# Block means of the first batch spread by POOL for both heads, and four weight pairs converted with the attention's priority

## Chip, cores, metric

One core of one Trainium2 chip runs the whole program. The time is device microseconds of one launch, median of the runs. Beside it stands one profiled execution, from which all rows below come. The engines are PE (TensorE: matmuls into PSUM), DVE (VectorE), ACT (ScalarE), POOL (GpSimd) and SP, which issues the DMAs.

## What is computed

For 4 batches: attention with 8 heads over 768 positions (head size 64), in which each query sees its neighbours within 16 positions and, beside them, 24 blocks of 32 positions: the maximum of each block's keys and the mean of its values. A mixer then works on the result (768 x 512 a batch): a product along the positions (768 to 256 to 768) that is added to its input, and one along the channels (512 to 1536 to 512) that is added again.

```python
k_sum = k.reshape(B, H, nb, block, D).max(axis=3)
v_sum = v.reshape(B, H, nb, block, D).mean(axis=3)      # the block means of this case
scores_l = where(|i - j| < 16, scale * q @ k.T, -1e9)
scores_s = scale * q @ k_sum.T + log(block)
a = softmax(concat([scores_l, scores_s]))
x = a @ concat([v, v_sum])                              # heads side by side: 768 x 512
u = x + (relu(x.T @ w_tok1) @ w_tok2).T
out = u + relu(u @ w_ch1) @ w_ch2
```

## The kernel before

**Stages.** Batch 0's attention runs alone in a start stage. Heads go in pairs `p` = 0 to 3: scores `sc` on PE, their lowest value on DVE (L481), the exponential `e` on ACT (L491), transposes `et` on PE, weighted sums `av` on PE, scaled by DVE into `x` (L610). Each pair's `x` goes through the first token product (`tok1`: PE into `t1p`, then ACT and DVE into `t1`, L734 and L739) and the second (`tok2`: PE into `up`, then ACT and DVE into `u`, L959 and L964). `u_0_1_2` is batch 0, second half of the positions, channel block 2. When the start is over, PE goes through a long stream of channel products, `hp` (L981, `ch1`) and `acc` (L1024, `ch2`), 24 steps a batch, with the attention of the next batch between the steps.

**Weights.** Single-precision weights are used as the sum of two shorter numbers, high and low, and are made on the chip in the start stage and the first stream. `w_tick(i)` takes pair `i`: two loads by SP, then ACT's absolute value (L1665), POOL's clamp (L1669), and on DVE a shift (L1674), a sign (L1681) and the low word (L1688); then, but for the first token weight, ACT writes the high part (L1712) and POOL subtracts to get the low part (L1718), twice each. Pairs 0 to 2 are `w_tok1` (tile `wt1`), 3 to 5 are `w_tok2` (`wb_3` to `wb_5`, into `wt2h` and `wt2l`), 6, 8, ... are `w_ch1` (`w1h`, `w1l`), 7, 9, ... are `w_ch2`. `tok2` needs all of 3 to 5; the stream's first step needs pair 6.

**Block means of batch 0.** `first_means(p)`: PE sums the 32 rows of each block in two parts for both heads into one PSUM bank (`vm`, tag `acc2`, of which there is one), ACT copies one part into `vs` (L372), DVE adds the other (L382), and 24 x 64 means must stand twelve times beside the values `v` as 24 x 768.

**Order.** Nothing is issued in the order of the code. Every piece of work is listed by `add(engine, estimated time, ..., rank)`, and `Plan._order` plays the list through with these estimates: each engine takes the ready piece of lowest rank, then of lowest place in the list. What comes out is a fixed order for each engine's queue; on the chip each engine keeps it and waits on semaphores. The ranks are `R_H, R_EVAC, R_ATT, R_LATER, R_W` = 0 to 4.

Of the kernel before, what the change touches and what calls it, by code (L numbers as in the profile page):

```python
# [15 lines left out]
ALU = mybir.AluOpType  # L16
# [3 lines left out]
B, H, S, D = 4, 8, 768, 64  # L20
# [5 lines left out]
NT = S // QT  # L26
NB = S // 32
WIN = 96
NC = WIN + NB
# [49 lines left out]
class Plan:  # L79
# [13 lines left out]
    def add(self, eng, took, run, reads=(), writes=(), rank=0, behind=(), kb=0):  # L93

        w = Work(len(self.works), eng, took, run, rank, kb)
        self.works.append(w)
        for key in reads:
            if key in self.wrote:
                w.needs.add(self.wrote[key])
            self.read[key].append(w)  # L100
        for key in writes:
            if key in self.wrote:
                w.needs.add(self.wrote[key])
            w.needs.update(self.read.pop(key, ()))
            self.wrote[key] = w
        for key in (*reads, *writes):
            s = getattr(key[0], "home", key[0])
            if isinstance(s, Slot) and (not s.users or s.users[-1] is not w):
                if not s.users:
                    w.takes.append(s)  # L110
                s.users.append(w)
        w.behind.update(behind)
        w.needs.discard(w)
        return w
# [85 lines left out]
def tile_attention_mixer(  # L200
# [13 lines left out]
    nc = tc.nc  # L214
# [6 lines left out]
    add = plan.add  # L221

    def sbuf(shape, tag, name, bufs, dtype=F32):
        return plan.slot(sb, shape, dtype, tag, name, bufs)
# [10 lines left out]
        out=means[:, NB - 2 : NB],  # L235
# [4 lines left out]
        out=means[:, NB - 2 : NB], in0=means[:, NB - 2 : NB], scalar1=1.0 / 32.0,  # L240
# [23 lines left out]
    R_H, R_EVAC, R_ATT, R_LATER, R_W = range(5)  # L264
# [11 lines left out]
    def bank(name, tags):  # L276
        tag = tags[turns[tuple(tags)] % len(tags)]
        turns[tuple(tags)] += 1
        return plan.slot(ps, [P, 512], F32, tag, name, 2 if tag in ("att", "mm") else 1)
# [8 lines left out]
    q_t, k_t, v_t, vs, vb_t = {}, {}, {}, {}, {}  # L288
# [62 lines left out]
    def first_means(p):  # L351

        pt = bank(f"vm_{p}", ["acc2"])
        s = sbuf([P, 2 * D], "vs", f"vs_0_{p}", 2)


        def sums():
            for t in range(NT):
                for j in range(2):
                    c = 2 * j + t % 2  # L360
                    nc.tensor.matmul(
                        pt.t[32 * c : 32 * c + NB, :D],
                        lhsT=means[:, NB - 2 - 2 * t : 2 * NB - 2 - 2 * t],
                        rhs=v_t[2 * p + j].t[:WIN, t], start=(t < 2), stop=(t >= NT - 2),
                    )

        def half(j, i):
            c = 2 * j + i
            return pt.t[32 * c : 32 * c + NB, :D]

        def first(j):
            nc.scalar.activation(s.t[WIN:NC, j * D : (j + 1) * D], half(j, 0), AF.Copy)  # L372

        def both(n):
            nc.vector.tensor_tensor(
                out=v_t[n].t[WIN:NC],
                in0=half(1, 1).unsqueeze(1).broadcast_to([NB, NT, D]),
                in1=s.t[WIN:NC, D:].unsqueeze(1).broadcast_to([NB, NT, D]), op=ALU.add,
            )

        def once():
            nc.vector.tensor_tensor(  # L382
                out=s.t[WIN:NC, :D], in0=half(0, 1), in1=s.t[WIN:NC, :D], op=ALU.add
            )

        def spread(n):
            nc.gpsimd.tensor_copy(
                v_t[n].t[WIN:NC], s.t[WIN:NC, :D].unsqueeze(1).broadcast_to([NB, NT, D])
            )

        add(
            "pe", 0.9, sums, reads=[(v_t[2 * p], 0), (v_t[2 * p + 1], 0)], writes=[(pt, 0)],
            rank=R_H,
        )
        for j in range(2):
            add(
                "act", 0.25, lambda j=j: first(j), reads=[(pt, 0)], writes=[(s, j)], rank=R_EVAC
            )
        add("dve", 0.2, once, reads=[(pt, 0)], writes=[(s, 0)], rank=R_EVAC)
        add(  # L400
            "pool", 0.95, lambda: spread(2 * p), reads=[(s, 0)], writes=[(v_t[2 * p], 1)],
            rank=R_ATT,
        )
        add(
            "dve", 0.95, lambda: both(2 * p + 1), reads=[(pt, 0), (s, 1)],
            writes=[(v_t[2 * p + 1], 1)], rank=R_EVAC,
        )

    def vb_load(b, c):
        tag, n, bufs = ("e", 16, 3) if b == 1 else ("vb", 8, 1)  # L410
# [233 lines left out]
    def att_step(b, s, behind=()):  # L644

        kind, hp, g = (LATER if b >= FAR else ORDER)[s]
        p = b * NP + hp
        if kind == "e":
            (turn_blocks if b >= FAR else turn)(p, g)
        elif kind == "a":  # L650
            weighted(p)
            if b >= FAR:
                turn_x(b, hp)
            ahead = 1 if b > 0 else 2
            if b > 0 or hp + ahead < NP:
                load_v(2 * (p + ahead))
                load_v(2 * (p + ahead) + 1)
        else:
            scores(p, g, behind)
            if b == 0 and g == 1:  # L660
                first_means(p)
            if g == 0 and p != NP - 1:
                key_blocks(p + 1)
            if g == 1 and p + 2 < (NP if b == 0 else B * NP):
                load_k(p + 2)
                state["q"] = load_q(p + 2)
# [929 lines left out]
    for i in range(3):  # L1596
        for k in range(2):
            cs, ws = slice(256 * i, 256 * (i + 1)), slice(512 * i, 512 * (i + 1))
# [12 lines left out]

    BUFS = {"u0": 4, "q": 2, "k": 2, "v": 2, "x": 2, "h": 2}
    ROOM = {"u0", "k", "h", "x"}
    TOKT = 3
    WTAGS = ["u0"] * 6 + ["k", "k", "q", "v", "x", "x"] * 4
    assert 2 * len(WTAGS) == len(jobs)

    def w_tick(i, behind=()):
# [12 lines left out]
        for j in range(2):  # L1631
# [7 lines left out]
            )  # L1639
        first, rank = two[0][1] is None, R_ATT if i < TOKT else R_W  # L1640
        psum = i >= 10
# [105 lines left out]
    for s in range(STEPS):  # L1747
# [4 lines left out]
        if ORDER[s][0] == "a":  # L1752
            p = ORDER[s][1]
# [143 lines left out]
```

## Time and profile before

| | |
|---|---|
| median of 3 runs | 560.84 us (560.51 to 561.32) |
| the profiled execution, its own time | 559.61 us |
| its span in the profile | 557.8 us |
| granted TensorE clock | 1.00 over the span |
| busy: PE, DVE, ACT, POOL | 544.0, 330.3, 251.9, 246.8 us |

The span is what the profile shows between the first and the last instruction; 1.8 us lie around it. A busy share is an average over stages: the start (to some 64 us) and the stream behind it have different limits. PE's busy time counts matmuls that overlap, so it is no measure of what could still be saved.

### The profile page before, as it was taken

How to read it: one execution, taken by the hardware profiler on the slowest of the kernel's cores; microseconds unless marked ns; L12 is line 12 of the kernel's file. 1: busy time of each engine (PE TensorE's matmuls, PEld its weight loads, DVE VectorE, ACT ScalarE, POOL GpSimd, SP SyncE). 2: the span in 40 equal slices, each digit the busy share in tenths (PEclk: the TensorE clock that was granted, in tenths of full speed). 3: DMA queues.
4: the chain of work that ended last, by engine and by line, in shares of the span. 5: the costliest groups of instructions: out<-in, count | busy, mean ns of one | idle time of the engine just before them, and what ended most of it. 6: DMA issues, size and time to landing. Idle time of an engine off the chain costs nothing.

```text
span 557.8 us, 12595 instructions
## 1 busy us (share of the span) xinstructions
PE 544.0 (98%) x4557; PEld 479.6 (86%) x4557; DVE 330.3 (59%) x922; ACT 251.9 (45%) x784; POOL 246.8 (44%) x362
## 2 busy tenths in 40 slices
PE   7699999999999999999999999999999999999997
PEld 4588788888999978888799988878889999999997
DVE  4788999979365355454543247454352065669992
ACT  4786666625585344332323325343433453356410
POOL 0326687835574932310067404378769963000000
PEclk9999999999999999999999999999999999999999
DMA  8963668755668138768595316787696543932742
GB/s 277 330 189 108 215 209 249 240 163 190 203 187 251 42 131 226 198 207 226 146 253 137 104 29 196 160 237 198 171 259 168 135 155 116 333 95 81 219 134 85
DMA packets 125743, 101.10 MB, mean 181 GB/s; under 512 B 70000, under 2 KB 105456, under 8 KB 125680
## 3 DMA queue, kind: packets, MB, share of 16 engines
q1 hardware_dynamic: 125680, 100.29, 60.7%
q8 instruction: 36, 0.59, 0.5%
q14 instruction: 27, 0.22, 0.1%
HBM read 70.18 MB, written 28.31 MB: 177 GB/s over the span
## 4 chain that ended last, share of the span: by engine, by line
PE 90%; ACT 4%; DVE 3%; POOL 2%; issue 1%; ACTq 0%
PE acc L1024 27%; PE hp L981 27%; PE sc L467 4%; PE av L599 4%; PE up L920 3%; PE t1q L837 3%; ACT e L491 2%; PE x L1251 2%; PE y L1251 2%; PE z L1251 2%; PE pz L1251 2%; PE t1q L800 2%; PE up L1213 2%; PE warm L1731 1%; PE pw L1251 1%; PE pv L1251 1%
## 5 line engine op out<-in xcount | busy, mean ns | idle before, releaser
L1024 PE MATMUL acc<-h,w2h 128*128 128x256 f32 (+1 forms) x576 | 153.8, 339 | 0.0
L981 PE MATMUL hp<-u,w1h 128*128 128x256 f32 (+1 forms) x576 | 143.8, 339 | 0.0
L1024 PEld LDWEIGHTS acc<-h,w2h 128*128 128x128 f32 x576 | 100.6, 188 | 13.8 <-ACT h L993 1.6
L981 PEld LDWEIGHTS hp<-u,w1h 128*128 128x128 f32 x576 | 98.0, 189 | 12.4 <-issue 1.1
L981 PE MATMUL hp<-u,w1l 128*128 128x256 f32 (+1 forms) x288 | 96.9, 336 | 0.0
L491 ACT ACTIVATE e<-e,den 128x120 f32<-128x120 f32 x192 | 73.3, 384 | 52.0 <-DVE den L481 39.1
L1024 PE MATMUL acc<-h,w2l 128*128 128x256 f32 (+1 forms) x288 | 96.4, 335 | 0.0
L998 DVE SCALAR_TENSOR_TENSOR h<-hp,h 128x512 fp32r<-128x512 f32 (+1 forms) x72 | 39.9, 554 | 90.9 <-ACT h L993 90.7
L993 ACT ACTIVATE h<-hp 128x512 fp32r<-128x512 f32 (+1 forms) x72 | 35.2, 489 | 114.7 <-PE hp L981 114.5
L981 PEld LDWEIGHTS hp<-u,w1l 128*128 128x128 f32 x288 | 54.4, 189 | 5.8
L1024 PEld LDWEIGHTS acc<-h,w2l 128*128 128x128 f32 x288 | 54.2, 188 | 5.2
L481 DVE CUSTOM_DVE_ANT_0 e<-sc,mask_sb 128x120 f32<-128x120 f32 x192 | 41.7, 277 | 16.8 <-PE sc L467 16.2
L605 POOL TENSOR_SCALAR rec<-den 128x6 f32<-128x6 f32 x32 | 8.6, 269 | 66.1 <-ACT e L491 64.0
L491 ACT ACTIVATION_READ_ACCUMULATOR e<-e,den 128x1 f32 x192 | 36.1, 188 | 0.0
L1064 POOL TENSOR_TENSOR ot<-ot,u 128x512 f32<-128x512 f32 (+1 forms) x24 | 24.4, 1042 | 19.7 <-DVE ot L1056 18.2
L467 PE MATMUL sc<-k,q 64*64 64x120 f32 x768 | 28.0, 271 | 3.7 <-DVE den L481 2.2
L467 PEld LDWEIGHTS sc<-k,q 64*64 64x64 f32 x768 | 20.5, 132 | 12.5 <-issue 6.2
L920 PE MATMUL up<-wt2h,t 128*128 128x512 f32 (+1 forms) x96 | 28.4, 354 | 0.6 <-DVE t L739 0.6
L599 PEld LDWEIGHTS av<-v,eT 120*64 120x64 f32 x768 | 24.0, 138 | 4.7 <-issue 2.8
L599 PE MATMUL av<-v,eT 120*64 120x64 f32 x768 | 26.5, 224 | 0.9 <-PE hp L981 0.4
L335 DVE TENSOR_REDUCE ks<-k 128x24 f32<-128x768 f32 x16 | 15.2, 948 | 20.5 <-DMA k<-in_kw 20.5
L423 DVE TENSOR_REDUCE vs<-vb 96x8 f32<-96x256 f32 (+1 forms) x40 | 17.8, 458 | 9.4 <-DMA vb<-in_vb 9.3
(248 smaller groups left out, 1042.7 us busy)
## 6 DMA issues: line engine op xcount, KB each, us to landing
w<-in_w_ch SPq DMA_DIRECT2D x48, 256.0 KB
k<-in_kw SPq DMA_DIRECT2D x16, 720.0 KB
v<-in_vw SPq DMA_DIRECT2D x32, 288.0 KB
q<-in_q SPq DMA_DIRECT2D x16, 384.0 KB
away<-e SPq DMA_DIRECT2D x16, 384.0 KB
eT<-away SPq DMA_DIRECT2D x64, 96.0 KB
w<-in_w_tok SPq DMA_DIRECT2D x12, 256.0 KB
vb<-in_vb SPq DMA_DIRECT2D x32, 96.0 KB
```

Source lines behind the costliest of these rows:

```text
L423: lambda: nc.vector.tensor_reduce(out=s.t[:VB, rows], in_=slot.t[:VB], axis=AX, op=ALU.add),
L467: nc.tensor.matmul(tiles[j].t[c * QT : (c + 1) * QT, i * NC : (i + 1) * NC], lhsT=qt.t[rows, t * QT : (t + 1) * QT], rhs=kt.t[rows, t, :], ...
L481: nc.vector.tensor_tensor_reduce(out=e.t[:, j, i * P : i * P + NC], in0=tiles[j].t[:, i * NC : (i + 1) * NC], in1=mask_sb[:, mv, :], op0=A ...
L491: nc.scalar.activation(ei, ei, AF.Exp, bias=den_t[n].t[:, 1, T : T + 1], scale=-1.0, accum_out=den_t[n].t[:, 0, T : T + 1],)
L599: nc.tensor.matmul(pv[cs, T], lhsT=eT[:NC, T % (TT // 2), cs], rhs=v.t[:NC, 2 * T + c], start=True, stop=True,)
L920: nc.tensor.matmul(pt.t[:, :nt], lhsT=t1.t[:, part, ks], rhs=w.t[:, k, h0 : h0 + nt], start=(far and k == 0 and i == 0), stop=(k == DTOK / ...
L981: nc.tensor.matmul(pt.t[:, :nt], lhsT=block(w, f, c), rhs=us[c].t[:, part], start=(i == 0), stop=(i == len(ops) - 1),)
L993: lambda: nc.scalar.activation(h.t[:, 0], pt.t[:, :nt], AF.Relu),
L998: lambda: nc.vector.scalar_tensor_tensor(out=h.t[:, 1], in0=pt.t[:, :nt], scalar=0.0, in1=h.t[:, 0].bitcast(F32), op0=ALU.max, op1=ALU.sub ...
L1024: nc.tensor.matmul(slot.t[:, c0 : c0 + nt], lhsT=block(w, f, o), rhs=h.t[:, part], start=(f == 0 and w == "w2h" and part == 0 and o % n == 0),
L1064: lambda view=view, u=u: nc.gpsimd.tensor_tensor(out=view(), in0=view(), in1=u.t[:, 1].bitcast(F32), op=ALU.add),
L1251: nc.tensor.matmul(pt.t[:, :cols], lhsT=w[wp][0](), rhs=z.t[:, zp], start=first and seen == 0, stop=final and seen == 3 * len(ops) - 1, sk ...
```

## The change

In `first_means` DVE no longer writes the second head's 24 x 768 itself (`both`, 24 x 768 from PSUM). It writes the 24 x 64 means of both heads (`once`), and POOL spreads both (`spread`, rank `R_ATT`). `TOKT` goes from 3 to 7: weight pairs 3 to 6 (the second token weight and the first pair of the first channel weight) get rank `R_ATT` in place of `R_W`, for all their steps on ACT, POOL and DVE.

```diff
-        def both(n):
+        def once(j):
+            cs = slice(j * D, (j + 1) * D)
             nc.vector.tensor_tensor(
-                out=v_t[n].t[WIN:NC],
-                in0=half(1, 1).unsqueeze(1).broadcast_to([NB, NT, D]),
-                in1=s.t[WIN:NC, D:].unsqueeze(1).broadcast_to([NB, NT, D]), op=ALU.add,
-            )
-        def once():
-            nc.vector.tensor_tensor(
-                out=s.t[WIN:NC, :D], in0=half(0, 1), in1=s.t[WIN:NC, :D], op=ALU.add
-            )
-        def spread(n):
+                out=s.t[WIN:NC, cs], in0=half(j, 1), in1=s.t[WIN:NC, cs], op=ALU.add
+            )
+        def spread(j):
             nc.gpsimd.tensor_copy(
-                v_t[n].t[WIN:NC], s.t[WIN:NC, :D].unsqueeze(1).broadcast_to([NB, NT, D])
+                v_t[2 * p + j].t[WIN:NC],
+                s.t[WIN:NC, j * D : (j + 1) * D].unsqueeze(1).broadcast_to([NB, NT, D]),
             )
...
-        add("dve", 0.2, once, reads=[(pt, 0)], writes=[(s, 0)], rank=R_EVAC)
-        add("pool", 0.95, lambda: spread(2 * p), reads=[(s, 0)], ..., rank=R_ATT)
-        add("dve", 0.95, lambda: both(2 * p + 1), reads=[(pt, 0), (s, 1)], ..., rank=R_EVAC)
+        for j in range(2):
+            add("dve", 0.2, lambda j=j: once(j), reads=[(pt, 0)], writes=[(s, j)], rank=R_EVAC)
+            add("pool", 0.95, lambda j=j: spread(j), reads=[(s, j)], ..., rank=R_ATT)
...
-    TOKT = 3
+    TOKT = 7
```

Since the order is played through anew, much of the start stage moves. Three places follow; line numbers of the changed kernel are 6 lower than before.

On DVE, at the means of pairs 0 and 1 (`vs_0_0`, `vs_0_1`; `e_1_1` are scores of pair 1, `ks_2` the block maxima of pair 2), before:

```order
L382 TENSOR_TENSOR vs_0_0_269<-vm_0_223,vs_0_0_269 24x64
L375 TENSOR_TENSOR v_1_89<-vm_0_223,vs_0_0_269 24x768
L481 ISA e_1_1_309,den_2_217<-sc_2_1_280,mask_sb_71 128x120
...
L610 TENSOR_TENSOR x_0_0_335<-av_0_296,rec_0_249 128x6x64
L335 TENSOR_REDUCE ks_2_363<-k_2_158 128x24
L610 TENSOR_TENSOR x_0_0_335<-av_1_318,rec_1_254 128x6x64
L382 TENSOR_TENSOR vs_0_1_376<-vm_1_338,vs_0_1_376 24x64
L375 TENSOR_TENSOR v_3_115<-vm_1_338,vs_0_1_376 24x768
```

and now:

```order
L376 TENSOR_TENSOR vs_0_0_269<-vm_0_223,vs_0_0_269 24x64 x2
L376 TENSOR_TENSOR vs_0_1_320<-vm_1_279,vs_0_1_320 24x64 x2
L604 TENSOR_TENSOR x_0_0_343<-av_0_307,rec_0_249 128x6x64
L335 TENSOR_REDUCE ks_2_358<-k_2_158 128x24
L344 COPY k_2_158<-ks_2_358 128x12x24
L604 TENSOR_TENSOR x_0_0_343<-av_1_345,rec_1_254 128x6x64
L475 ISA e_1_1_378,den_2_217<-sc_2_1_324,mask_sb_71 128x120
```

The means of pair 1 now stand directly behind those of pair 0, with nothing between them; `av` and the scores of pair 1 come later.

On POOL, from the clamp of `wb_3` to that of `wb_7` (`v_4` to `v_7` are the copies of pairs 2 and 3), before:

```order
L1669 TENSOR_SCALAR wb_3_578<-wb_3_578 128x512
L387 COPY v_4_333<-vs_0_2_588 24x768
L1669 TENSOR_SCALAR wb_4_626<-wb_4_626 128x512
L1718 TENSOR_TENSOR wt2l_705<-wb_3_578,wt2h_687 128x256 x2
L387 COPY v_6_532<-vs_0_3_703 24x768
L1669 TENSOR_SCALAR wb_5_745<-wb_5_745 128x512
L605 TENSOR_SCALAR rec_6_800<-den_6_629 128x6
L605 TENSOR_SCALAR rec_7_805<-den_7_631 128x6
L1718 TENSOR_TENSOR wt2l_705<-wb_4_626,wt2h_687 128x256 x2
L1718 TENSOR_TENSOR wt2l_705<-wb_5_745,wt2h_687 128x256 x2
L1669 TENSOR_SCALAR wb_6_854<-wb_6_854 128x512
```

and now:

```order
L381 COPY v_4_340<-vs_0_2_578 24x768
L381 COPY v_5_370<-vs_0_2_578 24x768
L1663 TENSOR_SCALAR wb_3_615<-wb_3_615 128x512
L1663 TENSOR_SCALAR wb_4_626<-wb_4_626 128x512
...
L1712 TENSOR_TENSOR wt2l_721<-wb_3_615,wt2h_714 128x256 x2
L381 COPY v_6_477<-vs_0_3_697 24x768
L381 COPY v_7_498<-vs_0_3_697 24x768
L1712 TENSOR_TENSOR wt2l_721<-wb_4_626,wt2h_714 128x256 x2
L1663 TENSOR_SCALAR wb_5_752<-wb_5_752 128x512
L1663 TENSOR_SCALAR wb_6_799<-wb_6_799 128x512
```

Two copies stand before the clamp of `wb_3`, two copies and the subtractions of `wb_4` before the clamp of `wb_5`, and the clamp of `wb_6` directly behind that of `wb_5`.

On DVE at the end of the start stage, where `t1` of pair 3 and the first `u` of the second half are made, before:

```order
L1688 SCALAR_TENSOR_TENSOR wb_8_914<-w_8_0_569,wb_8_914 128x256
L1688 SCALAR_TENSOR_TENSOR wb_8_914<-w_8_1_756,wb_8_914 128x256
L964 TENSOR_TENSOR u_0_1_0_973<-up_0_1_0_947,u_0_1_0_973 128x256
L964 TENSOR_TENSOR u_0_1_1_987<-up_0_1_1_962,u_0_1_1_987 128x256
L1674 TENSOR_SCALAR wb_9_958<-wb_9_958 128x512
L1681 SCALAR_TENSOR_TENSOR wb_9_958<-w_9_0_723,wb_9_958 128x256
L1681 SCALAR_TENSOR_TENSOR wb_9_958<-w_9_1_742,wb_9_958 128x256
```

and now:

```order
L1682 SCALAR_TENSOR_TENSOR wb_8_903<-w_8_0_509,wb_8_903 128x256
L1682 SCALAR_TENSOR_TENSOR wb_8_903<-w_8_1_749,wb_8_903 128x256
L1668 TENSOR_SCALAR wb_9_950<-wb_9_950 128x512
L733 SCALAR_TENSOR_TENSOR t1_0_3_966<-t1p_0_3_932,t1_0_3_966 128x256
L1675 SCALAR_TENSOR_TENSOR wb_9_950<-w_9_0_716,wb_9_950 128x256
L1675 SCALAR_TENSOR_TENSOR wb_9_950<-w_9_1_739,wb_9_950 128x256
L958 TENSOR_TENSOR u_0_1_0_986<-up_0_1_0_957,u_0_1_0_986 128x256
```

The shift and the two signs of `wb_9` now stand ahead of `u_0_1_0`.

## Rows read from the trace of the kernel before

**Rows 1.** From the page: the span, and the granted TensorE clock in 40 slices of it.

```profile
span 557.8 us, 12595 instructions
...
PEclk9999999999999999999999999999999999999999
```

**Rows 2.** Busy time of each engine (instructions in brackets) in the first stretch of the stream: start:end, length, PE, PEld, DVE, ACT, POOL, granted clock, DMA share, GB/s.

```profile
64.00:120.00 56.00, 56.00 (x269) 46.12 (x268) 53.10 (x96) 32.82 (x80) 42.30 (x62) 1.00 0.70 221
```

**Rows 3.** The chain of waits between 33 and 66 us, followed back from the stream's first product: start, length, what.

```profile
54.27 2.15 POOL w1l L1718 x2
...
61.67 0.42 DVE u L964
...
64.19 1.84 PE hp L981 x8
```

**Rows 4.** PE's instructions in order of time: start, length, line, operation, tiles, shape, count, and in brackets the idle time before it and what ended it.

```profile
60.71 0.73 PE L920 MATMUL up<-wt2h,t 128*128 128x512 f32 x2 [0.61 <-DVE t L739]
...
62.13 0.44 PE L912 MATMUL up<-identf,x 128*128 128x128 f32 x2 [0.22 <-DVE u L964]
...
64.02 0.63 PE L981 MATMUL hp<-u,w1h 128*128 128x512 f32 x2
```

**Rows 5.** Groups of instructions on DVE and POOL from 0 to 64 us: count, busy time, mean ns of one, idle time before them.

```profile
L375 DVE TENSOR_TENSOR v<-vm,vs 24x768 f32<-24x768 f32 x4 | 3.9, 965 | 0.1
...
L382 DVE TENSOR_TENSOR vs<-vm,vs 24x64 f32<-24x64 f32 x4 | 0.9, 221 | 2.4 <-ACT vs L372 2.3
...
L387 POOL COPY v<-vs 24x768 f32<-24x768 f32 x4 | 3.3, 824 | 6.3 <-DVE vs L382 6.0
```

**Rows 6.** The block means in order of time: DVE for pair 0, PE and ACT for pair 1, DVE for pair 2; columns as in rows 4.

```profile
15.62 0.22 DVE L382 TENSOR_TENSOR vs<-vm,vs 24x64 f32<-24x64 f32 x1 [1.08 <-ACT vs L372]
15.87 0.96 DVE L375 TENSOR_TENSOR v<-vm,vs 24x768 f32<-24x768 f32 x1
...
19.47 0.87 PE L361 MATMUL vm<-v,means 96*24 96x64 f32 x48
...
20.41 0.44 ACT L372 ACTIVATE vs<-vm 24x64 f32<-24x64 f32 x2 [0.97 <-PE vm L361]
...
35.81 0.22 DVE L382 TENSOR_TENSOR vs<-vm,vs 24x64 f32<-24x64 f32 x1 [0.53 <-ACT vs L372]
```

**Rows 7.** POOL in order of time, around the conversion of the second token weight; columns as in rows 4.

```profile
35.40 0.61 POOL L1669 TENSOR_SCALAR wb<-wb 128x512 f32<-128x512 f32 x1 [0.34 <-ACT wb L1665]
36.16 0.82 POOL L387 COPY v<-vs 24x768 f32<-24x768 f32 x1
...
41.17 1.66 POOL L1718 TENSOR_TENSOR wt2l<-wb,wt2h 128x256 fp32r<-128x256 f32 x2 [3.15 <-ACT wt2h L1712]
42.95 0.82 POOL L387 COPY v<-vs 24x768 f32<-24x768 f32 x1
43.86 0.61 POOL L1669 TENSOR_SCALAR wb<-wb 128x512 f32<-128x512 f32 x1
...
47.65 3.30 POOL L1718 TENSOR_TENSOR wt2l<-wb,wt2h 128x256 fp32r<-128x256 f32 x4
```

**Rows 8.** DVE in order of time, from the conversion of the second token weight to the end of the start stage; columns as in rows 4.

```profile
38.28 0.42 DVE L1674 TENSOR_SCALAR wb<-wb 128x512 int32<-128x512 int32 x1
...
39.47 0.69 DVE L1688 SCALAR_TENSOR_TENSOR wb<-w,wb 128x512 int32<-128x512 int32 x1
...
45.59 0.42 DVE L1674 TENSOR_SCALAR wb<-wb 128x512 int32<-128x512 int32 x1
46.68 0.19 DVE L625 RECIPROCAL rec<-rec 128x6 f32<-128x6 f32 x1 [0.67 <-POOL rec L605]
...
47.83 1.11 DVE L1688 SCALAR_TENSOR_TENSOR wb<-w,wb 128x512 int32<-128x512 int32 x1
...
51.57 0.43 DVE L1674 TENSOR_SCALAR wb<-wb 128x512 int32<-128x512 int32 x1 [1.69 <-POOL wb L1669]
52.03 0.98 DVE L1681 SCALAR_TENSOR_TENSOR wb<-w,wb 128x512 int32<-128x512 int32 x1
...
54.70 1.11 DVE L1681 SCALAR_TENSOR_TENSOR wb<-w,wb 128x512 int32<-128x512 int32 x1
...
57.73 0.69 DVE L964 TENSOR_TENSOR u<-up,u 128x512 fp32r<-128x512 f32 x1 [0.72 <-ACT u L959]
58.34 0.77 DVE L1674 TENSOR_SCALAR wb<-wb 128x512 int32<-128x512 int32 x1
59.14 1.18 DVE L1681 SCALAR_TENSOR_TENSOR wb<-w,wb 128x256 int32<-128x256 int32 x2
...
60.59 1.16 DVE L1688 SCALAR_TENSOR_TENSOR wb<-w,wb 128x256 int32<-128x256 int32 x2
61.67 0.74 DVE L964 TENSOR_TENSOR u<-up,u 128x256 fp32r<-128x256 f32 x2
62.33 1.00 DVE L1674 TENSOR_SCALAR wb<-wb 128x512 int32<-128x512 int32 x1
63.37 0.76 DVE L1681 SCALAR_TENSOR_TENSOR wb<-w,wb 128x256 int32<-128x256 int32 x2
```

**Rows 9.** SP's issue of the second group of token weight loads (six DMAs), and ACT's first use of them; columns as in rows 4.

```profile
21.12 7.41 SPq L1635 DMA_DIRECT2D w<-in_w_tok  x6
...
34.65 0.67 ACT L1665 ACTIVATE wb<-w 128x512 f32<-128x512 f32 x1
```

More of the change, by code (lines that the diff above doesn't have):

```diff
@@ L398, in first_means @@
             )
-        add("dve", 0.2, once, reads=[(pt, 0)], writes=[(s, 0)], rank=R_EVAC)
-        add(
-            "pool", 0.95, lambda: spread(2 * p), reads=[(s, 0)], writes=[(v_t[2 * p], 1)],
-            rank=R_ATT,
-        )
[L404 to L407, printed above, removed]
+        for j in range(2):
+            add(
+                "dve", 0.2, lambda j=j: once(j), reads=[(pt, 0)], writes=[(s, j)], rank=R_EVAC
+            )
+            add(
+                "pool", 0.95, lambda j=j: spread(j), reads=[(s, j)],
+                writes=[(v_t[2 * p + j], 1)], rank=R_ATT,
+            )
     def vb_load(b, c):
```

## Prediction

> **What bounds the kernel now.** I read the granted clock first: 1.00 in all slices [rows 1], so nothing below is a matter of TensorE's speed. Then the busy times by stretch, to see where PE is fed without a break: from 64 us on PE is busy 56.0 of 56.0 us [rows 2]. So the program is a start stage that ends with the stream's first product at 64.02 us [rows 4], and a stream that PE alone sets. The change touches the start stage; whatever the start gains or loses is passed on whole, as long as the stream stays fed.
>
> Then the chain of waits up to that product. It is not PE's: it goes through POOL's subtraction for the first `w1l`, pair 6 (54.27 us), and DVE's eviction of `u_0_1_0` (61.67 us), which frees the PSUM bank that PE's next `up` wants; PE runs from there to the product without a stop [rows 3]. PE's own rows say the same: it waits 0.61 us for DVE's `t1` and 0.22 us for that eviction, and the product starts 1.89 us after the second wait [rows 4]. So the question is when DVE reaches `u_0_1_0`. DVE's rows show how it got there: it waited three times for POOL or ACT (0.67, 1.69, 0.72 us), and several of its instructions took longer than the same ones elsewhere [rows 8].
>
> **The change, part by part.** I follow DVE from the block means to `u_0_1_0` in three legs.
>
> *The block means.* Each pair loses one `both` of 0.965 us and gains one more `once` of 0.22; POOL gains a copy of 0.82 [rows 5]. In DVE time that is 0.74 us a pair saved, 3.0 us for four. How much of it arrives? At pairs 0 and 1 the new order puts the two means side by side. The sums of pair 1 go to the one bank that the means of pair 0 read, so between the two stand PE's sums, 0.87 us, and ACT's copies, 0.44 us, and DVE waits out about 1.5 us with hand-overs, where before it had other work in that time [rows 6]. That takes pair 0's 0.74 us. At pair 2, the shift of `wb_3` started 2.47 us after the means (35.81 to 38.28) [rows 6, 8]. The order now has two copies and the clamp between them on POOL: 0.22 for the first mean, 2 x 0.82, 0.61 [rows 5, 7], with hand-overs 2.6 us. That takes pair 2's. Pair 1's 0.74 may survive; against it stands that ACT and PE have been handed another order. I take 0 for this leg, with POOL's first `wt2l` at 41.17 us as before [rows 7]; its bounds are -2.2 us (three pairs' savings kept) and +0.5 us.
>
> *POOL's queue to the clamp of `wb_5`.* From 41.17 us: the subtractions of `wb_3`, 1.66, to 42.83; two copies where one stood, 42.95 + 2 x 0.82 = 44.59; then the subtractions of `wb_4`, which stood behind the clamp and now stand ahead of it, two of the four that took 3.30, so 1.65, to 46.24; the clamp, 0.61, to 46.85 [rows 7]. DVE's shift of `wb_5` follows at 46.9 us, and it was at 45.59 [rows 8]: +1.3 us. The sign and low word of `wb_4`, 0.69 us each alone [rows 8], run on DVE at that time now, and may hold POOL up; no row prices it by itself. Between nothing and 0.8 us (twice the 0.4 us that DVE loses below) I take 0.3: +1.6 us, with bounds of +1.3 and +2.1.
>
> *DVE from the shift of `wb_5` to `u_0_1_0`.* Before, 45.59 to 61.67, that is 16.08 us [rows 8]. The same instructions stand there after the change, and three more: the shift and two signs of `wb_9`, which came behind. Unhindered these are 0.42 and 0.76 us [rows 8], overlapped ends taken off 1.14. A reciprocal of 0.19 us now stands right before each of the two products that need it: +0.2. The three waits of 0.67, 1.69 and 0.72 us, together 3.08, go away: the clamp of `wb_6` now stands directly behind that of `wb_5`, so the longest has no cause, and DVE reaches the other two later than what it waited for. That is -3.08, with a bound of -2.0 if the two smaller ones stay in part.
>
> Last, the hindrance. Six instructions of this leg were stretched: 1.11, 0.98, 1.11, 0.77 us where such a one takes 0.69, 0.69, 0.69 and 0.42 alone, and the two pairs 1.18 and 1.16 where such a pair takes 0.76 [rows 8]: 0.42 + 0.29 + 0.42 + 0.35 + 0.42 + 0.40 = 2.30 us, all while POOL worked. DVE had 3.08 us of pauses in which POOL's work cost nothing. Without them, some thirteen POOL instructions fall into a DVE queue with no gap; at 0.39 us each, the mean of the six, that would be 5.0 us in all. So the extra is between 0 and 2.7 us, and I take the middle, 1.35: DVE has sign, low word and shift of five weight pairs here, but the evictions between them read PSUM and were stretched nowhere.
>
> Here a rule speaks against the change. The rows show stretched conversions, and unstretched `both` and evictions (four `both`, all 965 ns [rows 5]). The Trainium skill (SBUF — State Buffer, section "SBUF: two separate sides") says that DVE and GpSimd share a port pair as an exclusive lock: a DVE instruction with two SBUF inputs or in a two-port mode, and a GpSimd instruction, block each other for a whole instruction. By it, `both` (PSUM and SBUF) never took the lock and each new copy does; if every added copy blocked a conversion in full, the sum would rise by 4 x 0.82 = 3.3 us, where the rows give 1.35. The copies of before overlapped no conversion, so no row here prices this meeting.
>
> *The loads.* `v_4` and `v_5` now bracket the loads of pair 3 of the keys in SP's queue, and `v_6`, `v_7` move ahead of two loads of `w_tok2`. Before, that group was issued by 28.5 us and first used at 34.65 us [rows 9]; six us cover a shift of two issues of some 0.5 us. I cost it at nothing; without that cover it would be 1 us on the leg before.
>
> The sum: 0 + 1.6 + (1.14 + 0.2 - 3.08 + 1.35) = +1.2 us at `u_0_1_0`, and as much at the stream's start, since PE waits there already. Against the profiled execution that is 559.6 + 1.2 = 560.8 us; this execution lies 1.2 us under the median of 560.84, so on the median's scale **562.1 us**.
>
> **The rivals.**
>
> *No change that shows.* The collisions on DVE are as many as before, POOL is held up by nothing, and the two smaller waits go too: 1.3 + 1.14 + 0.2 - 3.08 + 0.3 = -0.1 us, so 560.7. For it speaks that the start stage has three engines near their limit, so that work moved between them returns. Against it: DVE's queue without pauses must meet POOL more often.
>
> *Faster.* The savings on DVE before the first `wt2l` stay, up to 2.2 us, because the means of pair 1 hold up nothing that is needed soon; the rest is the rival above. Then the stream starts 1.5 to 2.3 us earlier: 558.5 to 559.3 us. It decides at one place: POOL's first `wt2l` must start before 40 us. For it: DVE is the engine on the chain, and it does 3 us less. Against it: the new order puts two POOL copies ahead of `wb_3`.
>
> *Slower by the port rule, or in the stream.* The collisions reach their upper bound (+2.7) and POOL its own (+2.1): 2.1 + 1.14 + 0.2 - 3.08 + 2.7 = +3.1, so 563.9 us. The same end is reached if the stream isn't fed: DVE is busy 53.1 of 56 us in its first stretch [rows 2], and a conversion that comes one slot late, some 1.9 us (38.28 to 39.47 + 0.69 [rows 8]), has little room to be made up there.
>
> **How the numbers follow.** A measurement of this kernel tells about 0.2% from no change, that is 1.1 us. The forecast's own case (+0.6 to +2.4 us) has a chance of 0.52, of which 0.12 lies under 1.1 us; no change 0.27; faster 0.12; the port rule or the stream 0.09. So slower 0.40 + 0.09 = 0.49, the same 0.27 + 0.12 = 0.39, faster 0.12. The range leaves out most of the faster case and the far end of the last: 560.0 to 563.7 us; the likeliest case alone is 561.4 to 563.2.
>
> **What the profile of the changed kernel would show.** POOL's first `wt2l` near 41 us, then two copies of 0.82 and the clamp of `wb_5` ending near 47; DVE without a pause over 0.5 us from there to `u_0_1_0`; that eviction at 62.5 to 63.5 us, PE waiting over 1 us for it, and the first `hp` product near 65.2. The means of pairs 0 and 1 with a DVE pause of 1.5 us between them. The prediction is wrong if the first `wt2l` comes before 40 us, if DVE keeps pauses of 2 us or more behind 47 us, or if PE waits for weights inside the stream.

## The result, and the profile after

| | before | after |
|---|---|---|
| median | 560.67 us (559.22 to 561.32, 6 runs) | 565.25 us (564.08 to 566.38, 6 runs) |
| profiled execution, its own time | 559.61 us | 564.08 us |
| span | 557.8 us | 562.3 us |
| granted clock over the span | 1.00 | 0.993 |
| first `hp` product | 64.02 us | 68.43 us |

The ratio is 1.0085, with a 95% interval of 1.0064 to 1.0106: slower by 4.6 us, where 1.2 were predicted and 563.7 us was the upper end of the range.

The page of the changed kernel, span and granted clock, to be held against [rows 1]:

```profile
span 562.3 us, 12606 instructions
...
PEclk9799999999999999999999999999999999999999
```

One slice, the second (14 to 28 us), shows 7 tenths; all others are as before. In windows of a tenth of a microsecond, PE alone (start:end, length, PE busy, granted clock, DMA share, GB/s):

```profile
18.40:18.50 0.10, 0.00 (x0) 0.53 1.15 430
...
25.20:25.30 0.10, 0.10 (x12) 0.83 1.06 430
```

The clock fell to its lower level (0.50, 1.2 GHz) at 18.4 us and was back at 25.2 us. What PE did around it, in order of time (start, length, line, operation, tiles, shape, count, idle time before and what ended it):

```profile
7.56 1.46 PE L461 MATMUL sc<-k,q 64*64 64x120 f32 x48
...
16.39 0.87 PE L361 MATMUL vm<-v,means 96*24 96x64 f32 x48 [1.61 <-ACT eT L534]
17.19 0.80 PE L593 MATMUL av<-v,eT 120*64 120x64 f32 x18
18.91 0.69 PE L593 MATMUL av<-v,eT 120*64 120x64 f32 x6 [0.92 <-issue]
19.52 1.48 PE L461 MATMUL sc<-k,q 64*64 64x120 f32 x24
20.93 1.55 PE L593 MATMUL av<-v,eT 120*64 120x64 f32 x24
22.41 1.62 PE L523 MATMUL et<-identf,e 128*120 128x128 f32 x6
...
47.12 0.54 PE L523 MATMUL et<-identf,e 128*120 128x128 f32 x3 [2.48 <-DVE x L604]
...
48.26 2.84 PE L747 MATMUL t1p<-x,wt 128*128 128x128 f32 x24
...
68.43 0.63 PE L975 MATMUL hp<-u,w1h 128*128 128x512 f32 x2
```

Ahead of the fall PE had waited 1.61 us for the one bank of the block sums (the profile names ACT's `eT`; the bank is free when DVE has made the means of pair 0, at 15.80 + 0.48 = 16.28 us), and then it stood 0.92 us in the middle of the weighted sums of head 0, for nothing that the profile shows; the fall came within that pause. Then the scores took 1.48 us where they take 0.85 at the upper level (19.80 us in e8's rows below), and the next two groups are as slow. The same place in the kernel before, whose order differs from there on:

```profile
7.38 1.46 PE L467 MATMUL sc<-k,q 64*64 64x120 f32 x48
...
17.31 1.50 PE L599 MATMUL av<-v,eT 120*64 120x64 f32 x43
19.15 0.39 PE L599 MATMUL av<-v,eT 120*64 120x64 f32 x5 [0.35 <-issue]
...
43.14 2.84 PE L753 MATMUL t1p<-x,wt 128*128 128x128 f32 x24
```

PE's busy time from that product of pair 2 to the stream, before and after (columns as in the windows above, instructions in brackets):

```profile
43.14:64.02 20.88, 19.74 (x176) 1.00 0.48 151
...
48.26:68.43 20.17, 19.57 (x176) 1.00 0.39 123
```

DVE and POOL after, for the places of [rows 6 to 8]:

```profile
15.80 0.48 DVE L376 TENSOR_TENSOR vs<-vm,vs 24x64 f32<-24x64 f32 x2 [1.08 <-ACT vs L372]
17.91 0.48 DVE L376 TENSOR_TENSOR vs<-vm,vs 24x64 f32<-24x64 f32 x2 [1.62 <-ACT vs L372]
...
37.63 0.48 DVE L376 TENSOR_TENSOR vs<-vm,vs 24x64 f32<-24x64 f32 x2 [0.30 <-ACT vs L372]
...
40.30 0.83 DVE L1668 TENSOR_SCALAR wb<-wb 128x512 int32<-128x512 int32 x1 [0.85 <-POOL wb L1663]
...
45.20 1.10 DVE L1682 SCALAR_TENSOR_TENSOR wb<-w,wb 128x512 int32<-128x512 int32 x1
...
49.88 0.43 DVE L1668 TENSOR_SCALAR wb<-wb 128x512 int32<-128x512 int32 x1 [0.84 <-POOL wb L1663]
...
60.65 1.71 DVE L1675 SCALAR_TENSOR_TENSOR wb<-w,wb 128x256 int32<-128x256 int32 x2
...
66.06 0.74 DVE L958 TENSOR_TENSOR u<-up,u 128x256 fp32r<-128x256 f32 x2
...
39.65 1.20 POOL L1663 TENSOR_SCALAR wb<-wb 128x512 f32<-128x512 f32 x2
...
43.88 1.86 POOL L1712 TENSOR_TENSOR wt2l<-wb,wt2h 128x256 fp32r<-128x256 f32 x2 [1.94 <-ACT wt2h L1706]
45.81 1.95 POOL L381 COPY v<-vs 24x768 f32<-24x768 f32 x2
...
49.23 0.61 POOL L1663 TENSOR_SCALAR wb<-wb 128x512 f32<-128x512 f32 x1
```

The table below puts the start stage in pieces, each taken between two of these rows: the first scores, the means of pair 2 (DVE, 35.81 us in [rows 6]), the shift of `wb_3`, POOL's first `wt2l`, the shift of `wb_5`, `u_0_1_0`, the first `hp` product. The last two columns are a run of the next section, the changed kernel with the clock held.

| piece, us | before | after | difference | e8 | e8 less before |
|---|---|---|---|---|---|
| start to first scores | 7.38 | 7.56 | +0.18 | 7.77 | +0.39 |
| to the means of pair 2 | 28.43 | 30.07 | +1.64 | 28.52 | +0.09 |
| to the shift of `wb_3` | 2.47 | 2.67 | +0.20 | 2.67 | +0.20 |
| to the first `wt2l` | 2.89 | 3.58 | +0.69 | 3.59 | +0.70 |
| to the shift of `wb_5` (leg 2) | 4.42 | 6.00 | +1.58 | 6.02 | +1.60 |
| to `u_0_1_0` (leg 3) | 16.08 | 16.18 | +0.10 | 16.18 | +0.10 |
| to the first `hp` product | 2.35 | 2.37 | +0.02 | 2.37 | +0.02 |
| sum | 64.02 | 68.43 | +4.41 | 67.12 | +3.10 |

Behind the product nothing is lost between these two executions: 557.8 - 64.02 = 493.8 us before, 562.3 - 68.43 = 493.9 after. In the profiled executions of the next section that part took 493.0 to 495.5 us; why it varies was not looked for.

### The profile page after: what moved, and what is told of

Same layout as the page of the kernel before. It is cut to its first block, busy times and chain, and to the rows that moved or that the text cites. A ratio compares the mean times of both kernels' runs of the same rounds, so it can differ in the third digit from the quotient of the medians.

```text
span 562.3 us, 12606 instructions
## 1 busy us (share of the span) xinstructions
PE 546.8 (97%) x4557; PEld 481.5 (86%) x4557; DVE 331.4 (59%) x922; ACT 252.7 (45%) x784; POOL 250.5 (45%) x366
## 4 chain that ended last, share of the span: by engine, by line
PE 87%; DVE 4%; DMA 3%; ACT 3%; SPq 1%; issue 1%; DVEq 0%
PE hp L975 26%; PE acc L1018 26%; PE av L593 4%; PE sc L461 4%; PE up L914 3%; PE t1q L831 3%; PE x L1245 2%; PE y L1245 2%; PE z L1245 2%; PE pz L1245 2%; ACT e L485 2%; PE t1q L794 2%; PE up L1207 1%; PE warm L1725 1%; PE et L523 1%; PE pw L1245 1%
## 5 line engine op out<-in xcount | busy, mean ns | idle before, releaser
L593 PE MATMUL av<-v,eT 120*64 120x64 f32 x768 | 27.9, 228 | 2.0 <-issue 0.9
L604 DVE TENSOR_TENSOR x<-av,rec 128x384 f32<-128x384 f32 x32 | 17.3, 552 | 14.6 <-PE av L593 13.1
```

The lines of the kernel that those rows point to most:

```text
L593: nc.tensor.matmul(pv[cs, T], lhsT=eT[:NC, T % (TT // 2), cs], rhs=v.t[:NC, 2 * T + c], start=True, stop=True,)
L604: nc.vector.tensor_tensor(out=x2.t[:, :, hp % 2, j * D : (j + 1) * D], in0=pt.t[:, : TT * D].rearrange("p (t d) -> p t d", d=D), in1=rec.t ...
```

## The experiments

Two questions: how much of the 4.4 us is the clock and how much the order of the work, and which part of the change brings it. All runs were timed beside the kernel before (medians of it 560.3 to 560.8 us).

**e1, e2, e3, e4: one pause filled; each part alone; a control.** The edits, against the changed kernel (e1, e2) and the kernel before (e3, and e4 with the edit of e1):

```diff
 # e1, e4
-                for i in range(TT // 2):
+                for i in [*range(TT // 2)] * (4 if (p, g, j) == (0, 1, 1) else 1):
 # e2
-    TOKT = 7
+    TOKT = 3
 # e3
-    TOKT = 3
+    TOKT = 7
```

e1: 

> The changed kernel with PE kept busy in one pause: the three transposes `et` of head 1, second half (pair 0), are made four times instead of once into the same bank, nine more instructions of about 0.13 us that should fill the pause of 1.6 us before the sums of pair 1 (14.77 to 16.39 us). The result is the same, since the last transposes write what the first wrote. Theory A (the granted clock, which stood at its lower level from 18.4 to 25.2 us, cost most of leg 1): the clock stays at 1.00, POOL's first `wt2l` comes back from 43.9 to 41 to 42 us, the first `hp` product from 68.4 to 65 to 66, and the time is 562 to 563 us. Rival B (the new order of PE, with the sums of pair 1 ahead of the weighted sums and the scores, costs it at any clock): the clock is back but the first `hp` product stays at 67.5 to 68.5 and the time at 564.5 to 565.5 us. If the clock falls all the same, the run says nothing of B.

e2: 

> Only the means spread by POOL for both heads; the priority of the weight pairs as before (three pairs). The order of PE up to the stream is that of the changed kernel. Theory A: the clock falls at 18 us as in the changed kernel, and the time is 563 to 565.5 us, so the first part of the change alone brings most of the loss. Rival C (the four weight pairs with the attention's priority are what delays the start): the clock is at 1.00, and the time is 560 to 561.5 us.

e3: 

> Only the priority of the weight pairs; the means are made as before. The order of PE up to 30 us is that of the kernel before. Theory A: clock 1.00, and a time within 1.5 us of the kernel before (559.5 to 562). Rival C: 563 to 565.5 us at a clock of 1.00.

e4: 

> The kernel before with the same nine added transposes, as a control of e1: they should lie in a pause of PE of 1.3 us (14.85 to 16.16 us). Both theories: clock 1.00, 560 to 561.3 us. If it is slower by more than 0.5 us, the added transposes cost something themselves, and e1 has to be read less by that.

| | median, us | ratio, interval | mean clock of its executions |
|---|---|---|---|
| e1 | 565.70 | 1.0104 (1.0080 to 1.0127) | 0.993 to 0.994 |
| e2 | 567.53 | 1.0134 (1.0112 to 1.0157) | 0.988 to 0.991 |
| e3 | 564.58 | 1.0079 (1.0051 to 1.0106) | 0.990 to 0.994 |
| e4 | 561.35 | 1.0023 (1.0003 to 1.0042) | 0.990 to 0.997 |

e1 could not tell the theories apart: the clock held at 18 us and fell elsewhere, from 13.7 to 17.1 and from 47.8 to 51.2 us. PE in e1: the filled transposes, and the first token product behind a pause of 2.48 us, 4.47 us long where it takes 2.84 at the upper level:

```profile
15.95 2.40 PE L523 MATMUL et<-identf,e 128*120 128x128 f32 x15
...
46.47 0.54 PE L523 MATMUL et<-identf,e 128*120 128x128 f32 x3 [2.48 <-DVE x L604]
...
47.61 4.47 PE L747 MATMUL t1p<-x,wt 128*128 128x128 f32 x24
```

The control did not come out as expected either: the kernel before, filled in the same way, ran its transposes at the lower level (15 of them in 3.46 us, where 15 took 2.40 in e1, 1.1 us of that at the lower level too), and its executions went from 560.3 to 564.6 us:

```profile
15.48 3.46 PE L529 MATMUL et<-identf,e 128*120 128x128 f32 x15
```

So the clock isn't a property of the changed order alone. The executions of the kernel before beside these four runs show it: of 17, the two with a mean clock of 1.00 took 558.8 and 559.1 us, those with 0.993 to 0.996 took 559.5 to 562.2, and the three with 0.988 took 561.7 to 562.6. The profiled execution of before, from which the prediction was made, was one with 1.00.

Each part alone is slower than the kernel before, and their losses (6.9 and 3.9 us) don't add up to 4.6. Neither came out as expected: e2 lies above both of its ranges, and e3 in rival C's, but with a clock that fell twice. In e2 POOL's first `wt2l` comes at 49.58 us, and PE waits 3.66 us for DVE's first `u` before its last `t1p`; the clock falls once more in that wait, and the product takes 4.57 us. In e3, PE's `av` of pair 2 stands behind a wait that the profile puts down to POOL's `wt2l`, for 2.30 us, and the product starts at 68.21:

```profile
62.55 4.57 PE L747 MATMUL t1p<-x,wt 128*128 128x128 f32 x24 [3.66 <-DVE u L958]
```

```profile
45.08 1.62 PE L599 MATMUL av<-v,eT 120*64 120x64 f32 x48 [2.30 <-POOL wt2l L1718]
```

**e5, e6, e7: the pauses filled.** Products of the warm-up's own operands into the warm-up's bank are put where PE waits. The text of the expectations gives the places; the code is

```diff
+    def fill(*key):
+        for _ in range(FILL.get(key, 0)):
+            nc.tensor.matmul(pw.t, lhsT=warm.t[:, :P], rhs=warm.t, start=True, stop=True)
```

with a call behind the scores and the transposes and within the first token product (so the line numbers of the filled kernels are some 6 to 15 higher).

e5: 

> The changed kernel with PE kept busy in most of its pauses of the start stage: products of the warm-up's own operands into the warm-up's bank (0.24 us each) where PE waits (2 behind the scores of pair 0, 1 and 2 at its first transposes, 5 before the sums of pair 1, 3 at the transposes of pair 1, 4 in the first token product), and 15 transposes of the identity into unused columns of the last scores' bank. No result depends on them. Theory A (about half of the loss is the granted clock, which falls where PE waits; at the upper level the change costs the +1.2 us that was predicted): the mean clock is above 0.995, and the time is 1 to 2 us over the same kernel of before with its pauses filled (e6). Rival B (the new order costs the whole 4.6 us at any clock): the mean clock is above 0.995 and the time 3.5 to 5 us over e6.

e6: 

> The kernel before with the same filling in its own pauses of the start stage (2, 1, 2, 4 as in e5, 6 before the scores of pair 1, 3 and 4 in the first token product). Both theories: the mean clock is above 0.995. Of the kernel before, executions with a mean clock of 1.00 took 558.8 to 559.6 us and those with 0.988 to 0.994 took 559.5 to 562.6. So A and B expect 558.5 to 559.8 us, if the added products cost nothing themselves.

e7: 

> Only the priority of the weight pairs (e3), with the filling of e6. In e3 the clock fell twice in the start stage (12.9 to 16.3 and 30.0 to 33.4 us) and the first `hp` product came at 68.2 us. Theory A: with the clock held the time is within 1.5 us of e6. Rival B (the order behind 40 us, where PE waited 2.3 us for POOL's `wt2l`, costs it at any clock): 2.5 to 4 us over e6.

| | median, us | ratio, interval | mean clock |
|---|---|---|---|
| e5 | 563.77 | 1.0047 (1.0028 to 1.0066) | 0.997 to 1.00 |
| e6 | 560.06 | 0.9986 (0.9965 to 1.0007) | 0.999 to 1.00 |
| e7 | 563.22 | 1.0054 (1.0030 to 1.0079) | 0.993 to 1.00 |

e5 lies 3.7 us over e6, in rival B's range, but its clock wasn't held: the three executions at 1.00 took 561.5 to 562.1 us, which is A's range, the two at 0.999 took 563.6 and 563.7, the six at 0.997 took 563.8 to 565.7. e6 held it, and 56.77 us lie between its first scores and the first product (56.64 before). Yet its median lies 0.3 us above what both theories expected, and 1.2 us above the four executions of the kernel before beside it that had a clock of 1.00 (558.7 to 559.7 us, median 558.8). Either filling costs something, or the executions that keep 1.00 unfilled are fast for another reason too; no run tells which. So those are to be held against one another: e5's three lie 2.9 us above these four (median 561.8).

```profile
8.34 1.46 PE L473 MATMUL sc<-k,q 64*64 64x120 f32 x48
...
65.11 0.63 PE L996 MATMUL hp<-u,w1h 128*128 128x512 f32 x2
```

e7: the three executions at 1.00 took 562.8 to 563.7 us, about 3 over e6. So the priority of the weight pairs alone costs some 3 us with the clock at its upper level, as rival B said; three executions are few, and one of the other four, at 0.997, took 561.95 us.

**e8: the clock held. e9: the old order of PE.** e8 fills two products more, where e5 still fell:

```diff
-FILL = {..., ("et", 1, 1, 2): 5, ...}
+FILL = {..., ("et", 1, 1, 2): 7, ...}
```

e9 is the changed kernel, without filling, and with

```diff
+    state["vm", 1].behind.add(state["av", 1])
     plan.write()
```

e8: 

> As e5, with two more products of the warm-up (7 instead of 5) before the sums of pair 1, the place where e5 still paused 0.53 us ahead of the pause of 1.05 us in its weighted sums (PE waited there for nothing that the profile shows, in the changed kernel 0.92 us from 17.98 on) and where its clock fell at 19.2 us. Theory A: no fall any more in the start stage, mean clock 0.999 to 1.00, the first `hp` product 57.5 to 58.5 us behind the first scores (56.6 in the kernel before, 60.9 in the changed one, 60.6 in e5), and 561.3 to 562.3 us. Rival B: clock 0.999 to 1.00, but 60 to 61 us from the first scores to the product, and 563.5 to 565 us.

e9: 

> The changed kernel, with one constraint for the order: PE's sums of pair 1 (`vm`) may not start before the weighted sums of head 1, so that PE's order up to 25 us is that of the kernel before; behind it the order is played through anew. Theory A (the sums of pair 1 moved ahead bring PE to the gap in its instructions earlier and to more pauses, and so the fall at 18.4 us and a late first half of the start stage): the pause behind 17 us is 0.4 us or less, the clock holds from 17 to 25 us, and POOL's first `wt2l` comes 33.5 to 34.5 us behind the first scores (36.3 in the changed kernel, 33.8 before); the time is 561 to 563 us. Rival B (not that place): `wt2l` 35.5 us or more behind the first scores with the clock at its upper level, 564 to 566 us.

e8 took 562.96 us, ratio 1.0047 (1.0028 to 1.0066), with a clock of 0.999 to 1.00 in all six executions. Its rows in order of time:

```profile
7.77 1.46 PE L467 MATMUL sc<-k,q 64*64 64x120 f32 x48
...
17.38 0.45 PE L606 MATMUL av<-v,eT 120*64 120x64 f32 x6
19.07 0.80 PE L606 MATMUL av<-v,eT 120*64 120x64 f32 x18 [1.25 <-issue]
19.80 0.85 PE L467 MATMUL sc<-k,q 64*64 64x120 f32 x24
...
67.12 0.63 PE L990 MATMUL hp<-u,w1h 128*128 128x512 f32 x2
...
36.29 0.48 DVE L376 TENSOR_TENSOR vs<-vm,vs 24x64 f32<-24x64 f32 x2 [0.30 <-ACT vs L372]
...
38.96 0.82 DVE L1683 TENSOR_SCALAR wb<-wb 128x512 int32<-128x512 int32 x1 [0.86 <-POOL wb L1678]
...
48.57 0.43 DVE L1683 TENSOR_SCALAR wb<-wb 128x512 int32<-128x512 int32 x1 [0.85 <-POOL wb L1678]
...
64.75 0.74 DVE L973 TENSOR_TENSOR u<-up,u 128x256 fp32r<-128x256 f32 x2
...
42.55 1.88 POOL L1727 TENSOR_TENSOR wt2l<-wb,wt2h 128x256 fp32r<-128x256 f32 x2 [1.95 <-ACT wt2h L1721]
```

From the first scores to the first product it takes 59.35 us, between what A (57.5 to 58.5) and B (60 to 61) expected: neither is the whole. The table above divides it. Up to the means of pair 2 the changed kernel lost 1.55 us more than e8 (30.07 against 28.52), and that is the only piece in which they differ. With the clock held, that piece takes what it took before (28.52 against 28.43), and the new order costs 0.20 + 0.70 + 1.60 + 0.10 + 0.02 = 2.6 us behind it. The 0.09 is a net: against the first scores, the second part of the first token product of pair 0 starts 1.67 us later than before (31.77 and 29.71 us), but the sums of pair 2 now follow directly on it, where `av` stood between them.

e9 took 562.83 us, ratio 1.0045 (1.0030 to 1.0061). The weighted sums of pair 0 run without a pause and `wt2l` comes 34.32 us behind the first scores, as A expected and 0.5 us later than before, although the clock stood at the lower level from 11.9 to 18.7 us; so a fall doesn't cost the same at every place. But the order behind it changed too, and there the gain went: PE waited 2.57 us before the weighted sums of head 3, by the profile for the scores' minima on DVE, and the product came 59.61 us behind the first scores:

```profile
7.69 1.46 PE L461 MATMUL sc<-k,q 64*64 64x120 f32 x48
...
18.77 1.62 PE L593 MATMUL av<-v,eT 120*64 120x64 f32 x48
...
30.05 0.92 PE L593 MATMUL av<-v,eT 120*64 120x64 f32 x24 [2.57 <-DVE den L475]
...
67.30 0.63 PE L975 MATMUL hp<-u,w1h 128*128 128x512 f32 x2
...
42.01 2.27 POOL L1712 TENSOR_TENSOR wt2l<-wb,wt2h 128x256 fp32r<-128x256 f32 x2 [0.66 <-ACT wt2h L1706]
```

**e10: the copies moved behind the clamp.** Leg 2 tried on e8:

```diff
+    for j in (0, 1):
+        state["spread", 3, j].behind.add(state["clamp", 5])
     plan.write()
```

> e8 (the changed kernel with PE's pauses filled), and one constraint for the order: POOL's two copies of the means of pair 3 may not start before the clamp of `wb_5`. On POOL that clamp then stands directly behind the subtractions of `wb_3`, and the two copies behind those of `wb_4`. PE's order up to the stream's first steps is that of e8. Theory L2 (the two copies and the subtractions ahead of the clamp are leg 2's 1.6 us, and it arrives whole at the stream): from POOL's first `wt2l` to DVE's shift of `wb_5` 4.4 us or less (6.0 in the changed kernel and in e8, 4.4 before), the first `hp` product 57.5 to 58.0 us behind the first scores (59.35 in e8), the time 561 to 561.8 us. Rival D (DVE's queue behind it is full, so an earlier clamp only moves the wait): the product 58.8 us or more behind the first scores, 562.5 to 563.5 us.

e10 took 564.42 us, ratio 1.0079 (1.0063 to 1.0095), at a clock of 0.999 to 1.00: 1.5 us slower than e8, and 0.9 us over the upper end of what rival D expected.

```profile
46.41 0.95 DVE L1683 TENSOR_SCALAR wb<-wb 128x512 int32<-128x512 int32 x1 [0.32 <-POOL wb L1678]
...
59.32 1.01 DVE L617 TENSOR_TENSOR x<-av,rec 128x384 f32<-128x384 f32 x2
...
7.38 1.46 PE L467 MATMUL sc<-k,q 64*64 64x120 f32 x48
...
60.38 2.94 PE L762 MATMUL t1p<-x,wt 128*128 128x128 f32 x24 [1.48 <-DVE x L617]
...
68.67 0.63 PE L990 MATMUL hp<-u,w1h 128*128 128x512 f32 x2
```

L2 is half right. The shift of `wb_5` came 3.88 us behind the first `wt2l` (6.02 in e8), so the two copies and the subtractions of `wb_4` were what held it. But the gain did not arrive, and more was lost: with the conversion of `wb_5` earlier on DVE, five of the minima of pair 3's scores came behind it, the copies that its weighted sums need ended at 50.4 us, DVE's `x` of pair 3 started only at 59.32 us and PE's last `t1p` waited 1.48 us for it. The product came 61.29 us behind the first scores. PE's order isn't that of e8 either, as the expectation had it: two groups of `up` (49.00 and 52.85 us) stand ahead of the weighted sums of pair 3 now. So e10 did not try leg 2 alone.

**e11, e12: a shorter warm-up.** e6 with 16 and with 12 products of warm-up in place of 21.

```diff
-        for _ in range(21):
+        for _ in range(16):     # e12: 12
```

e11: 

> The kernel before with its pauses filled (e6), and 16 products of warm-up instead of 21. The warm-up ended between 7.4 and 8.6 us in the profiled executions so far, at whatever place the clock rose, while the keys were ready at 6.2 us in the kernel before. If the first scores wait for nothing but the warm-up, they start 1 to 2 us earlier and the time is 558.3 to 559.3 us, below e6 (560.06) and the kernel before. If the loads or DVE's key maxima hold them, or if the clock rises later for it, it stays at 559.7 to 560.5 us.

e12: 

> As e11 with 12 products of warm-up. The first scores then wait for the keys (6.2 us) and no more is to be had than in e11; if the clock has not risen by then, the scores run at the lower level and the time is that of e6 or above: 559 to 561 us.

Both beat both kernels: 558.99 us, ratio 0.9976 (0.9967 to 0.9985), and 558.59 us, ratio 0.9971 (0.9960 to 0.9983). e11 came out as expected, e12 0.4 us below the 559 to 561 us that were expected of it if the clock had not risen by then. In e12 the first scores start at 6.40 us (6.89 in e11). A shorter warm-up without the filling was not run.

## Why the prediction was wrong, point by point

**What bounds the kernel: right.** Everything was lost before the first product, +4.41 of +4.5 us of the span, and the stream kept its length to 0.1 us between the two executions.

**"It is not PE's … So the question is when DVE reaches `u_0_1_0`": half of it.** DVE's way adds up, but PE's queue beside it was as tight. From the first token product of pair 2 to the stream PE was idle for 1.14 of 20.88 us before and for 0.60 of 20.17 after (0.61 of 20.18 in e8), over the same 176 instructions. With this order of PE, then, legs 2 and 3 could give back no more than 0.6 us at the product. The loss lies on the way to that product of pair 2, which came 5.12 us later (48.26 and 43.14 us), 3.80 in e8. Half of that is one wait, 2.48 us for DVE's `x` of pair 2. Its weighted sums were done at 43.86 us; ahead of its reciprocal stood the sign and the low word of `wb_4`, 1.26 and 1.10 us, which now have the reciprocal's rank. The sum has no term for it. And PE did not wait "over 1 us" for `u_0_1_0`: it waited 0.37 us for `t1` and went on. This too is read from the rows; no run took the wait alone.

**"So nothing below is a matter of TensorE's speed": wrong, and half of what was missing.** This step read one execution. The clock of the kernel before stood at 1.00 in it, and below that in most of the executions that were timed later; that the profiled one lay 1.2 us under the median was in the sum, and it was not asked why. For the changed kernel the level fell at 18.4 us and cost 1.55 us up to the means of pair 2. The medians say the same: 565.25 - 562.96 = 2.3 us between the changed kernel and e8, 0.2 to 0.7 us between the kernel before and e6; so 1.6 to 2.1 us of the 4.6 go with the clock, and e8 less e6, 2.9 us, is the order (2.6 by the rows).

**Leg 1, "I take 0, with the first `wt2l` at 41.17 us": the term that failed.** It came at 43.88, +2.71, far beyond the bound of +0.5: 0.18 from the first scores, 1.64 up to the means of pair 2, of which 1.55 the clock, and 0.89 behind them. The means of pairs 0 and 1 stood 1.62 us apart on DVE, as said (1.5), and the savings of DVE did vanish there: e8 has +0.09. The shift of `wb_3` came 2.67 us behind the means (2.6 said). Not seen was what follows it, taken over from before as 2.89 us and now 3.58. The clamp of `wb_4` stands directly behind that of `wb_3` (the two from 39.65 to 40.85), and the shift of `wb_3` beside it took 0.83 us, where it took 0.42 [rows 8]; the other 0.28 us lie between the low word and POOL's start, where ACT's two copies of the block sums of pair 3 (42.92 us, 0.44) now stand ahead of the first high part, which came first before. This is read from the rows; no run took it alone, but in e9, where POOL has the sums `rec` in the place of the second clamp, the shift took 0.43 us (39.01).

**Leg 2, +1.6: right on DVE's way.** +1.58, and +1.60 in e8. The clamp of `wb_5` ended at 49.84 and not near 47 since leg 1 came late. e10 shows that what stands ahead of the clamp is the cause, and the replayed order gave nothing back; PE's queue, above, left 0.6 us to gain.

**Leg 3, -0.4: right in its steps, a little low.** No pause of DVE over 0.5 us was left. The hindrance was +1.8 where +1.35 was taken, bounds 0 to 2.7: nine instructions or pairs were stretched between 49.88 and 66.06 us (0.98, 1.20, 1.12, 1.12, 1.05, 0.96 and the pairs 1.71, 1.16, 0.95), 4.10 us over what they take alone, against 2.30 before. So 1.14 + 0.2 - 3.08 + 1.8 = +0.1.

The rule that the prediction weighed here (the Trainium skill, SBUF — State Buffer, section "SBUF: two separate sides": an exclusive lock on the port pair of DVE and GpSimd) would have made the added copies the cost. The two copies from 45.81 to 47.76 us met the end of one low word (1.10 us) and then reciprocals, products and minima of DVE, which took their usual 0.18, 0.56 and 0.27 us; the longest stretch, 1.71 us for a pair of 0.76, lay beside POOL's subtraction from 60.2 us on. The rule bears on the conversions, and these copies hardly met any.

**The loads, 0: right.** SP issued the last token weight at 32.1 us, and ACT used the first of that group at 38.38. The profile's chain of waits names two loads between 22.56 and 31.13 us, but DVE stood idle before neither of the instructions that it puts behind them (27.16 and 31.18 us).

**The rivals.** "Faster" decided at a first `wt2l` before 40 us, and that was refuted as the text said. The stream was fed. The case that came, slower by more than 0.2%, had 0.49, but it went beyond every rival (the farthest was 563.9 us) and by mechanisms that were none: PE's own clock, and PE's wait for an `x` behind a conversion. Neither of the first two signs of being wrong that the text named came (`wt2l` before 40 us; a DVE pause of 2 us behind 47 us), and the stream kept its length.

## What to carry to other kernels

Before a start stage is summed up from one profiled execution, see whether the clock in it is that of the median execution, and whether PE has pauses that the new order lengthens or joins; filling them with idle products shows what the clock is worth once it holds (the second try here), if both kernels are filled, and filling them with a shorter warm-up was here the better change (0.9971). Where a list scheduler replays the order, a part of the change can't be costed alone: each part lost 4 and 7 us by itself, both together 4.6, and a repair of the worst leg (e10) moved the wait to another input of the same product. A piece that is taken over "as before" needs its rows under the new neighbours too: beside a clamp directly behind another one, the shift that everything waits for took twice its time. And a chain that runs through one engine is to be held against the idle time of the next: where that is 0.6 us, no more can come back.

## What the runs showed of the hardware

**PE's clock in one program differs from execution to execution.** The kernel before took 558.8 us at a mean of 1.00 and 562.6 at 0.988. In the profiled executions with 21 products of warm-up the first scores started between 7.38 and 8.60 us, though everything ahead of them is the same: the 21 products took 6.28 to 7.50 us, the first of them longer than the last. (The profile's clock reads 1.00 in this time, so the rise itself shows only in their length.) The Trainium skill (TensorE: Matmul & The Clock Gate, section "Part 1: The HAM clock gate") says that the period over which the activity is judged runs by itself and doesn't begin with the kernel, so that the moment of the rise varies; these starts agree with it.

**PE pauses at a fixed place in its instructions.** The pause without a cause in the profile lay behind 18 instructions of `av` in the changed kernel, behind 8 in e5, which has 10 products more ahead of it, and behind 6 in e8, which has 12 more: each added product moves it by one. In the order of before it lay behind 43, in e6 with 9 products more behind 34, in e11 with 4 more behind 39, in e12 with as many as before again behind 43. Counted from the first product of the warm-up, that is 219 or 220 products in all nine traces that have the pause. It ended at 18.91 us in the changed kernel, and at 19.07 in e8, though it began earlier there; e1 and e9, which reached `av` at 19.07 and 18.77 us, had none. So the pause looks like instructions that arrive late. The traces speak for it: between 12 and 19 us the instruction queue (q8 of the page) moves one packet, of 16 KB, from 16.45 to 17.55 us in the changed kernel; its end lies between 17.14 and 18.45 us in the nine traces, and the pause ends 1.3 to 1.6 us behind it in each. It was not tried by an experiment. What the pause costs by itself no run separates (1.25 us of it lie on the chain of waits in e8); in the changed kernel the clock fell in it.
